# Seven block products instead of eight for the second half of a Mish layer, and two small jobs moved from ScalarE to VectorE

## The chip, the cores and the metric

The kernel runs on one core of one Trainium2 chip. The metric is the device time of one execution in microseconds (us). The kernel before takes 588.06 us, the median of three runs (586.24 to 589.32).

## What is computed

```python
def reference(q, k, v, w_a, w_b, w_out, w_in2, w_out2):   # shortened
    # q, k, v: 2 batches, 8 heads, 576 tokens, 64 per head, float32
    x = softmax(rotate(q) @ rotate(k).T / 8) @ v          # to 1152 tokens x 512
    x = ((x @ w_a) * (x @ w_b)) @ w_out                   # 512 -> 1536 -> 512
    h = x @ w_in2                                         # 512 -> 2048
    g = h * tanh(log1p(exp(min(h, 20))))                  # Mish
    return g @ w_out2                                     # 2048 -> 512
```

## The kernel before

The program has four parts that run into each other: attention of batch 0, attention of batch 1 beside the gated layer of batch 0 (`layer1`, `layer2`), the gated layer of batch 1, and the last layer, which the change is mostly about. Matmuls whose operands need float32 accuracy are done in three passes (`PASSES`): each operand is split into a high and a low part, by a cast or a scaled cast on ScalarE and a subtraction on VectorE, and high x high, high x low and low x high are added up in PSUM.

**The last layer.** The 1152 tokens are two groups: group 0 has 512 tokens, group 1 has 640 (64 of batch 0 and all of batch 1). d_ff = 2048 is cut into 16 tiles `f` of 128. `hidden(g, f)` loads a w_in tile, splits it (ScalarE `w`, VectorE `w`), multiplies it with the split y into a PSUM tile `h` of `h_ps` (two buffers), applies Mish on ScalarE and splits the result into `g`. For group 0 that is 12 matmuls of 512 columns, for group 1 two halves of 320 tokens with 12 matmuls each. `accumulate(g, f)` runs four steps later (`LAG4`): it splits a w_out tile and adds `g` x w_out into PSUM tiles `acc` (six buffers in `acc_ps`), 12 matmuls of 512 columns for group 0 and 15 for group 1. In group 0 the w_out tiles still come as 64-bit words; VectorE turns them into float32 with a shift and two passes (`xw`), and `magnitude` on ScalarE sums the absolute values of each (`junk`, with a read of the accumulator), from which a power of two for w_out's half-precision split in group 1 is made. Tiles converted earlier are kept in DRAM and come back as `wc`.

**The order.** Nothing is issued as it is written. Every call is recorded with a due time (`at`), and `Plan.order` then lists the instructions of each engine by due time and readiness with prices of its own; `any_` lets it choose VectorE or GpSimd. It also keeps VectorE and GpSimd instructions on SBUF operands apart (`lock`). Each engine works through its list strictly in order. All DMAs are issued by SyncE.

**The quotients.** `finish` divides the weighted sums `o` of attention by the softmax denominators `den`. For batch 1 (`p >= NP`) VectorE makes the reciprocals and ScalarE multiplies, two instructions per tile of tokens (`xn`), and two for the rest of 64 tokens (`xbd`).

All traced instructions carry one line (L397, where the plan issues them), so groups are told apart by the names of tiles.

Of the kernel before, what the change touches and what calls it, by code (L numbers as in the profile page):

```python
# [467 lines left out]
def kernel(ctx: ExitStack, tc: tile.TileContext, qk, v5, w1, w2, w34, tab, out):  # L468
# [711 lines left out]

# [22 lines left out]
    acc_t = {}  # L1203

    def hidden(g, f, t0, step):

# [11 lines left out]
        gt = t_p.tile([128, 2, 1280 if g else 640], F16 if g else F32R, tag="g", name=f"g{g}_{f}", bufs=GB)
        for hf in range(nt // hw):
            at(t0 + step * hf * hw / nt)  # L1220
            h = h_ps.tile([128, 512], F32, tag="h", name=f"h{g}_{f}_{hf}")[:, :hw]
# [14 lines left out]
            if g:
                act.activation(gt[:, 0, gs], h, AF.Copy, scale=g_up)
                dve.scalar_tensor_tensor(gt[:, 1, gs], h, g_up, gt[:, 0, gs], op0=ALU.mult, op1=ALU.subtract)
                continue
# [110 lines left out]
```

## Time and profile before

| | |
|---|---|
| median of three runs | 588.06 us |
| profiled execution, span | 588.73 us, 586.9 us |
| TensorE (PE) busy | 562.3 us (96%) |
| VectorE (DVE) busy | 435.1 us (74%) |
| ScalarE (ACT) busy | 380.6 us (65%) |
| GpSimd (POOL) busy | 110.0 us (19%) |
| mean granted TensorE clock | 0.990 of 2.4 GHz |

The span runs from the first to the last instruction of the profiled execution; about 1.8 us of its time lie around it. Busy shares are means over parts with different limits, so the stretches are to be read one by one. An instruction's duration includes some latency that the next one on its engine overlaps, so two neighbours can start closer together than their durations say.

### The profile page before, as it was taken

Reading aid. Unit: us, or ns where it says so; the run is one execution under the profiler, and the core shown is the slowest. Engines: PE = TensorE matmul, PEld = TensorE weight load, DVE = VectorE, ACT = ScalarE, POOL = GpSimd, SP = SyncE. Lnnn points to the kernel's source line nnn. Section 1 sums busy time; section 2 is a strip of 40 time slices with the busy share of each in tenths; the row PEclk is TensorE's granted clock in tenths of the full one; section 3 lists DMA queues with packets and bytes.
Section 4 is the critical chain, followed back from the end, with each engine's and each line's share of the span. In section 5 each row is a group of like instructions: output and inputs, shape, how many; then the busy total and the mean of one; then the engine's idle time right before and its main releaser. Section 6 shows DMA issues by size and latency. Waiting matters only on the chain.

```text
span 586.9 us, 11417 instructions
## 1 busy us (share of the span) xinstructions
PE 562.3 (96%) x4318; PEld 433.8 (74%) x4318; DVE 435.1 (74%) x822; ACT 380.6 (65%) x775; POOL 110.0 (19%) x122
## 2 busy tenths in 40 slices
PE   7899899899998999999999999999989999999997
PEld 5678678798887898889777789965656576655553
DVE  4788999799999989986999999468767625433231
ACT  3889678577776775553876644269999946554430
POOL 3774674415513231200000000000000000000000
PEclk9999999899998999999999999999999999999999
DMA  8246155599997998899999955033763204420002
GB/s 321 85 127 235 55 189 160 159 192 269 266 188 205 266 243 177 190 207 351 402 337 317 291 197 180 6 120 132 263 228 132 90 0 167 158 89 2 1 0 90
DMA packets 84391, 104.02 MB, mean 177 GB/s; under 512 B 51440, under 2 KB 53232, under 8 KB 84336
## 3 DMA queue, kind: packets, MB, share of 16 engines
q1 hardware_dynamic: 84336, 103.29, 58.8%
q8 instruction: 34, 0.56, 0.4%
q14 instruction: 21, 0.17, 0.1%
HBM read 74.94 MB, written 17.04 MB: 157 GB/s over the span
## 4 chain that ended last, share of the span: by engine, by line
PE 66%; ACT 16%; DVE 9%; DMA 4%; issue 3%; POOL 0%; SPq 0%; ACTq 0%; DVEq 0%; POOLq 0%
PE l L397 32%; PE acc L397 11%; PE h L397 9%; PE s L397 6%; ACT L397 5%; PE o L397 4%; DMA pt<-pp 4%; ACT w L397 2%; DVE xw L397 2%; DVE m L397 2%; PE tm L397 2%; ACT junk L397 2%; ACT h L397 1%; ACT g L397 1%; ACT e L397 1%
## 5 line engine op out<-in xcount | busy, mean ns | idle before, releaser
L397 PE MATMUL l<-x,w 128*128 128x320 f32 (+3 forms) x1152 | 160.9, 297 | 2.7 <-DVE a_sb L397 1.8
L397 PEld LDWEIGHTS <-w 128*128 128x128 f16 x1152 | 111.4, 98 | 58.1 <-issue 8.8
L397 DVE SCALAR_TENSOR_TENSOR xw<-wr,xw 128x512 uint32<-128x512 uint32 x160 | 120.1, 759 | 1.2
L397 PE MATMUL acc<-w,g 128*128 128x512 f16 (+1 forms) x432 | 104.6, 393 | 0.0
L397 PE MATMUL h<-y,w 128*128 128x320 f16 (+1 forms) x576 | 99.1, 326 | 3.0 <-DVE g L397 2.4
L397 PEld LDWEIGHTS l<-x,w 128*128 128x128 f32 x576 | 80.2, 195 | 7.8 <-issue 3.4
L397 PE MATMUL l<-ab,w 128*128 128x320 f32 (+1 forms) x576 | 81.8, 298 | 0.1
L397 PEld LDWEIGHTS l<-ab,w 128*128 128x128 f32 x576 | 77.3, 188 | 1.2 <-issue 0.8
L397 DVE TENSOR_REDUCE m<-s 128x1 f32<-128x576 f32 x72 | 51.9, 751 | 12.0 <-PE s L397 11.7
L397 DVE SCALAR_TENSOR_TENSOR w<-wc,w_up,w 128x512 f16<-128x512 f32 x56 | 41.6, 750 | 17.9 <-ACT w L397 17.8
L397 ACT ACTIVATE junk<-xw 128x512 f32<-128x512 f32 x56 | 35.4, 632 | 22.4 <-DVE xw L397 22.1
L397 ACT CAST w<-xw 128x512 fp32r<-128x512 f32 x64 | 39.5, 617 | 15.4 <-DVE xw L397 15.0
L397 PE MATMUL s<-qk 64*128 64x288 f32 x256 | 46.4, 444 | 2.9 <-DVE qk L397 1.5
L397 DVE TENSOR_TENSOR w<-xw,w 128x512 fp32r<-128x512 f32 x50 | 38.5, 770 | 14.0 <-ACT w L397 13.9
L397 ACT ACTIVATE h<-h,h_dn 128x320 f32<-128x320 f32 (+1 forms) x48 | 26.7, 555 | 28.2 <-PE h L397 27.9
L397 ACT ACTIVATE w<-wc,w_up 128x512 f16<-128x512 f32 x56 | 39.5, 716 | 6.4 <-PE l L397 3.0
L397 PEld LDWEIGHTS <-g 128*128 128x128 f16 x240 | 23.5, 98 | 26.4
L397 PEld LDWEIGHTS acc<-w,g 128*128 128x128 f32 x192 | 35.8, 188 | 9.2
L397 DVE SCALAR_TENSOR_TENSOR g<-h,g_up,g 128x320 f16<-128x320 f32 x32 | 17.6, 549 | 29.9 <-ACT g L397 29.9
L397 DVE TENSOR_SCALAR xw<-wr 128x512 uint32<-128x512 uint32 x80 | 35.8, 458 | 1.8 <-DMA wr<-in_w_dram 1.6
L397 PEld LDWEIGHTS s<-qk 64*128 64x128 f32 x256 | 25.3, 190 | 12.1 <-issue 4.8
L397 ACT ACTIVATE s<-s,m 128x576 f32<-128x576 f32 x36 | 25.1, 716 | 12.1 <-DVE m L397 11.6
(134 smaller groups left out, 760.8 us busy)
## 6 DMA issues: line engine op xcount, KB each, us to landing
wr<-in_w_dram SPq DMA_DIRECT2D x80, 512.0 KB, 4.8
wc<-kc SPq DMA_DIRECT2D x48, 256.0 KB, 3.4
kc<-xw SPq DMA_DIRECT2D x32, 256.0 KB, 3.2
qkr<-in_qk_dram SPq DMA_DIRECT2D x14, 576.0 KB, 5.5
ka<-xw SPq DMA_DIRECT2D x24, 256.0 KB, 3.1
wc<-ka SPq DMA_DIRECT2D x24, 256.0 KB, 6.2
v<-in_v_dram SPq DMA_DIRECT2D x12, 320.0 KB, 4.8
out_dram<-o_sb SPq DMA_DIRECT2D x9, 256.0 KB, 2.2
```

The source lines that it names most:

```text
L397: getattr(engine, method)(*map(real, args), **{k: real(v) for k, v in kw.items()})
```

## The change

Three things change.

1. Group 1's hidden layer is made by pairs of w_in tiles (`hidden_two`). With the 640 tokens cut in halves, the 512 rows of k in halves and two tiles of w_in side by side, h is a product of 2 x 2 by 2 x 2 blocks. It is now formed with seven block products and sums of blocks around them. Sums of y blocks are made once, by GpSimd, and split (`token_sums`); sums of w_in blocks are made for each pair by GpSimd (`wx`) and split together with the first tile and half of the second (`wv`). The seven products go to PSUM (`h_ps`, and a new buffer `z_ps` for products 2 and 5), and VectorE adds them up in an SBUF tile `hb`, one copy being ScalarE's. Mish and the split of g then work on 640 tokens at once, from SBUF. `acc_ps` has five buffers instead of six. The scale of y in batch 1 is lowered by four, and g's bound follows.
2. The magnitude of w_out in group 0 is a maximum of absolute values on VectorE (`top`) in place of ScalarE's sum.
3. The quotients of batch 1 are formed on VectorE, one instruction of 128 columns per tile of tokens and two for the rest.

```diff
@@ weights
+            if top is not None:
+                dve.tensor_reduce(top, r, axis=AX.X, op=ALU.max, apply_absolute_value=True)
@@ finish
-        if rest and p >= NP:
-            for i in range(2):
-                r = slice(64 * i, 64 * i + 64)
-                act.activation(xbd[p % 2][r, r], oo[r, i], AF.Copy, scale=den[r, i : i + 1])
-            return
         if rest:
             for i in range(2):
                 r = slice(64 * i, 64 * i + 64)
                 eng.tensor_tensor(xbd[p % 2][r, r], oo[r, i], den[r, i : i + 1].to_broadcast([64, D]), op=ALU.mult)
             return
...
-        if p >= NP:
-            for i in range(2):
-                act.activation(xn_t[p, part][:, c, i], oo[:, i], AF.Copy, scale=den[:, i : i + 1])
-            return
         eng.tensor_tensor(xn_t[p, part][:, c], oo, den.unsqueeze(2).to_broadcast([128, 2, D]), op=ALU.mult)
@@ tile_attention_moe_kernel
-    acc_cm, acc_ps = open_pool("acc_ps", 6, side="right", space=PSUM)
+    acc_cm, acc_ps = open_pool("acc_ps", 5, side="right", space=PSUM)
+    z_cm, z_ps = open_pool("z_ps", space=PSUM)
...
+    def token_sums(t0):
+        def a(r, c):
+            return [y32[1][2 * c + i][:, 0, 320 * r : 320 * r + 320] for i in range(2)]
...
+        for x, y, z, op in (
+            (s1, a(1, 0), a(1, 1), ALU.add),
+            (s2, s1, a(0, 0), ALU.subtract),
+            (s3, a(0, 0), a(1, 0), ALU.subtract),
+        ):
+            for i in range(2):
+                pool.tensor_tensor(x[i], y[i], z[i], op=op)
+        def split(t, i):
+            x = t_p.tile([128, 2, 640], F16, tag=f"sp{i}", name=f"sp{i}")
+            f = t.rearrange("p m n -> p (m n)")
+            act.activation(x[:, 0], f, AF.Copy, scale=y_up[:, 1:2])
+            dve.scalar_tensor_tensor(x[:, 1], f, y_up[:, 1:2], x[:, 0], op0=ALU.mult, op1=ALU.subtract)
+            return x
...
+    def hidden_two(f, t0, step, y):
+        at(t0 - W_LEAD)
+        r = []
+        for i in range(2):
+            x = rings["rawc"][0].tile([128, 512], F32, tag="rawc", name=f"wt{f}_{i}", bufs=rings["rawc"][1])
+            sp.dma_start(x, kept[f"c{2 * (f + i)}"])
+            r.append((x[:, 0:256], x[:, 256:512], x))
+        (b11, b21, b1), (b12, b22, _) = r
+        t = rings["raw"][0].tile([128, 512], I64, tag="raw", name=f"wx{f}", bufs=rings["raw"][1])
...
+        pool.tensor_tensor(t1, b12, b11, op=ALU.subtract)
+        pool.tensor_tensor(t3, b22, b12, op=ALU.subtract)
+        pool.tensor_tensor(t2, b22, t1, op=ALU.subtract)
+        pool.tensor_tensor(t4, b21, t2, op=ALU.subtract)
...
+        for w, x, c in ((wb, b1, slice(0, 512)), (wb, b22, slice(512, 768)), (wt, t, slice(0, 1024))):
+            act.activation(w[:, 0, c], x, AF.Copy, scale=up)
+            dve.scalar_tensor_tensor(w[:, 1, c], x, up, w[:, 0, c], op0=ALU.mult, op1=ALU.subtract)
...
+        def product(k, w, c, a):
+            at(t0 + step * k / 7)
+            ps, tag = (z_ps, "z") if k in (2, 5) else (h_ps, "h")
+            h = ps.tile([128, 512], F32, tag=tag, name=f"h1_{f}_{k}")[:, :320]
+            for i in range(2):
+                for n, (ws, xs) in enumerate(PASSES):
+                    lhsT = w[:, ws, c + 128 * i : c + 128 * i + 128]
+                    pe.matmul(h, lhsT=lhsT, rhs=a(i, xs), start=(i == n == 0), stop=(i == 1 and n == 2))
+            return h
...
+        act.copy(h11, product(0, wb, 0, y_part(0, 0)))
+        add(h12, product(1, wt, 256, s_part(1)), h11)
+        add(h11, product(2, wb, 256, y_part(0, 1)), h11)
+        add(h22, product(3, wt, 512, s_part(2)), h12)
+        add(h21, product(4, wt, 768, y_part(1, 1)), h22)
+        h = product(5, wt, 0, s_part(0))
+        add(h22, h, h22)
+        add(h12, h, h12)
+        add(h12, product(6, wb, 512, s_part(3)), h12)
+        gt = [t_p.tile([128, 2, 1280], F16, tag="g", name=f"g1_{f + i}", bufs=GB) for i in range(2)]
+        for i in range(2):
+            h, g = hb[:, 2 * i : 2 * i + 2].rearrange("p a b -> p (a b)"), gt[i]
+            act.activation(h, h, AF.Mish, scale=dn)
+            act.activation(g[:, 0, 0:640], h, AF.Copy, scale=g_up)
+            dve.scalar_tensor_tensor(g[:, 1, 0:640], h, g_up, g[:, 0, 0:640], op0=ALU.mult, op1=ALU.subtract)
+        return gt
@@ accumulate
-            stat=None if g else 2 * NF1 + NF2 + f,
+            top=None if g else o_sum[:, f : f + 1],
@@ the loop over steps
-            g_t[q] = hidden(*steps[q], T, d)
+            g, f = steps[q]
+            if not g:
+                g_t[q] = hidden(g, f, T, d)
+            elif f % 2 == 0:
+                g_t[q], g_t[q + 1] = hidden_two(f, T, 2 * d, groups[1][3])
+        if q == S_AT:
+            token_sums(T)
```

How the change moves instructions is shown at three places. In the names the number behind a tile's letters is the instance: `h0_6` is the hidden tile 6 of group 0, `h1_0_1` product 1 of pair 0, `wv2` and `wx2` the splits and differences of the pair that begins with tile 2, `xw117` a w_out tile being converted.

On ScalarE, in the middle of group 0, there stood before:

```order
L397 ACT_TABLE_LOAD
L397 ACTIVATE junk44_6042,o_sum_5516<-xw101_6004 128x512
L397 CAST w101_6049<-xw101_6004 128x512
L397 ACT_TABLE_LOAD
L397 ACTIVATE h0_5_0_6020<-h0_5_0_6020,h_dn_5738 128x512
L397 ACTIVATE w106_6060<-wc106_5811,w_up_3543 128x512
L397 CAST g0_5_6068<-h0_5_0_6020 128x512
```

and now:

```order
L397 CAST w99_6077<-xw99_6044 128x512
L397 ACTIVATE h0_6_0_6052<-h0_6_0_6052,h_dn_5721 128x512
L397 ACTIVATE w108_6089<-wc108_5816,w_up_3529 128x512
L397 CAST g0_6_6095<-h0_6_0_6052 128x512
L397 CAST w101_6103<-xw101_6066 128x512
L397 ACTIVATE h0_7_0_6105<-h0_7_0_6105,h_dn_5721 128x512
```

The magnitude and the two table loads around it are gone from the step.

On VectorE, at the end of group 0, there stood before:

```order
L397 TENSOR_TENSOR g0_14_6502<-h0_14_0_6474,g0_14_6502 128x512
L397 TENSOR_TENSOR w121_6515<-xw121_6396,w121_6515 128x512
L397 SCALAR_TENSOR_TENSOR w126_6534<-wc126_6242,w_up_3543,w126_6534 128x512
L397 TENSOR_TENSOR g0_15_6539<-h0_15_0_6513,g0_15_6539 128x512
L397 TENSOR_TENSOR w123_6551<-xw123_6441,w123_6551 128x512
L397 SCALAR_TENSOR_TENSOR g1_0_6572<-h1_0_0_6548,g_up_5876,g1_0_6572 128x320
```

and now:

```order
L397 TENSOR_REDUCE o_sum_4134<-xw117_6459 128x1
L397 TENSOR_TENSOR w117_6488<-xw117_6459,w117_6488 128x512
L397 TENSOR_TENSOR g0_14_6495<-h0_14_0_6451,g0_14_6495 128x512
L397 SCALAR_TENSOR_TENSOR wv2_1_6453<-wx2_6418,two_up_5716,wv2_1_6453 128x1024
L397 TENSOR_SCALAR xw118_6519<-wr118_6468 128x512
L397 SCALAR_TENSOR_TENSOR wv4_0_6502<-wt4_0_6227,two_up_5716,wv4_0_6502 128x512
L397 SCALAR_TENSOR_TENSOR xw118_6519<-wr118_6468,xw118_6519 128x512
L397 TENSOR_TENSOR g0_15_6537<-h0_15_0_6510,g0_15_6537 128x512
L397 SCALAR_TENSOR_TENSOR xw118_6519<-wr118_6468,xw118_6519 128x512
L397 TENSOR_SCALAR xw119_6553<-wr119_6493 128x512
L397 TENSOR_REDUCE o_sum_4134<-xw118_6519 128x1
L397 TENSOR_TENSOR hb0_6580<-h1_0_1_6563,hb0_6580 128x320
```

The reduces and the splits of the pairs 2 and 4 stand among the low parts of g, and the conversion of the last w_out tiles now ends behind the first sum of pair 0.

On VectorE, in the middle of group 1, a pair now looks so (there was one split of g and one of a weight per half before):

```order
L397 TENSOR_TENSOR hb8_7083<-h1_8_4_7136,hb8_7083 128x320
L397 TENSOR_TENSOR hb8_7083<-h1_8_5_7146,hb8_7083 128x320 x2
L397 SCALAR_TENSOR_TENSOR g1_8_7161<-hb8_7083,g_up_6041,g1_8_7161 128x640
L397 SCALAR_TENSOR_TENSOR w129_7178<-wc129_6957,o_up_6781,w129_7178 128x512
L397 TENSOR_TENSOR hb8_7083<-h1_8_6_7175,hb8_7083 128x320
L397 SCALAR_TENSOR_TENSOR wv14_0_7188<-wt14_0_6980,two_up_5716,wv14_0_7188 128x512
L397 SCALAR_TENSOR_TENSOR wv14_0_7188<-wt14_1_6985,two_up_5716,wv14_0_7188 128x256
L397 TENSOR_TENSOR hb10_7201<-h1_10_1_7203,hb10_7201 128x320
```

The splits for pair 14 stand between the sums of two neighbouring pairs.

## Rows read from the trace of the kernel before

**Rows 1.** Windows of each engine, with the columns in the first line.

```profile
core 0: us, PE busy (x) PEld busy (x) DVE busy (x) ACT busy (x) POOL busy (x), PEclk, DMA share, GB/s
388.50:409.00 20.50, 20.50 (x94) 10.95 (x93) 16.95 (x38) 19.58 (x33) 0.00 (x0) 1.00 0.30 98
409.00:466.70 57.70, 55.19 (x241) 34.10 (x241) 39.27 (x65) 56.85 (x86) 0.00 (x0) 1.00 0.55 186
489.40:583.00 93.60, 93.48 (x539) 53.33 (x539) 33.48 (x57) 42.65 (x77) 0.00 (x0) 1.00 0.21 70
120.00:270.00 150.00, 144.86 (x1354) 129.78 (x1353) 139.13 (x261) 99.06 (x225) 41.42 (x35) 0.99 0.95 226
```

**Rows 2.** Timeline of PE in w_in/w_out stage: start us, us, instruction.

```profile
403.60 2.76 PE L397 MATMUL h<-y,w 128*128 128x512 f16 x12
...
409.01 2.76 PE L397 MATMUL h<-y,w 128*128 128x512 f16 x12
...
466.73 1.79 PE L397 MATMUL h<-y,w 128*128 128x320 f16 x12
...
498.29 3.42 PE L397 MATMUL h<-y,w 128*128 128x320 f16 x24
501.55 3.40 PE L397 MATMUL acc<-w,g 128*128 128x512 f16 x15
504.79 3.42 PE L397 MATMUL h<-y,w 128*128 128x320 f16 x24
```

**Rows 3.** Timeline of ACT, one step of group 0.

```profile
447.11 0.66 ACT L397 ACTIVATE h<-h,h_dn 128x512 f32<-128x512 f32 x1
...
448.90 1.28 ACT L397 ACT_TABLE_LOAD   x1
450.19 0.63 ACT L397 ACTIVATE junk<-xw 128x512 f32<-128x512 f32 x1
...
451.44 1.28 ACT L397 ACT_TABLE_LOAD   x1
452.74 0.66 ACT L397 ACTIVATE h<-h,h_dn 128x512 f32<-128x512 f32 x1
```

**Rows 4.** Timeline of DVE, three neighbours in group 0.

```profile
417.27 0.42 DVE L397 TENSOR_SCALAR xw<-wr 128x512 uint32<-128x512 uint32 x1
417.61 1.29 DVE L397 SCALAR_TENSOR_TENSOR xw<-wr,xw 128x512 uint32<-128x512 uint32 x2
418.81 0.75 DVE L397 SCALAR_TENSOR_TENSOR w<-wc,w_up,w 128x512 f16<-128x512 f32 x1
```

**Rows 5.** Groups by form, DVE, 20 to 110 us: xcount | busy us, mean ns.

```profile
L397 DVE SCALAR_TENSOR_TENSOR xw<-wr,xw 128x512 uint32<-128x512 uint32 x11 | 11.9, 1081 | 0.0
...
L397 DVE TENSOR_SCALAR xw<-wr 128x512 uint32<-128x512 uint32 x6 | 4.5, 762 | 0.0
```

**Rows 6.** Groups by form, DVE, 388 to 466 us.

```profile
L397 DVE SCALAR_TENSOR_TENSOR xw<-wr,xw 128x512 uint32<-128x512 uint32 x26 | 17.8, 689 | 0.5
```

**Rows 7.** Groups by form, whole span, GpSimd and DVE.

```profile
L397 POOL TENSOR_TENSOR ab<-a_sb,ab 128x256 fp32r<-128x256 f32 x12 | 10.3, 855 | 42.1 <-ACT ab L397 42.1
...
L397 DVE TENSOR_REDUCE m<-s 128x1 f32<-128x576 f32 x72 | 51.9, 751 | 12.0 <-PE s L397 11.7
...
L397 DVE TENSOR_TENSOR ab<-l,ab 128x320 fp32r<-128x320 f32 x12 | 5.9, 488 | 0.0
...
L397 DVE SCALAR_TENSOR_TENSOR y<-y,y_up 128x320 f16<-128x320 f32 x8 | 4.0, 549 | 0.0
...
L397 DVE SCALAR_TENSOR_TENSOR y<-y,y_up 128x512 f16<-128x512 f32 x4 | 2.7, 746 | 0.0
```

**Rows 8.** Groups by form, ACT, 110 to 270 us; idle before it behind the bar.

```profile
L397 ACT ACTIVATE xn<-o,den 128x64 f32<-128x64 f32 x32 | 8.3, 312 | 6.3 <-DVE den L397 6.2
```

**Rows 9.** Windows as in rows 1, around a drop of the clock.

```profile
180.00:185.00 5.00, 3.58 (x14) 2.08 (x13) 3.79 (x8) 2.44 (x8) 0.89 (x2) 0.81 1.00 302
185.00:190.00 5.00, 5.00 (x36) 5.00 (x35) 5.00 (x9) 3.16 (x6) 0.88 (x1) 0.85 0.46 96
```

More of the change, by code (lines that the diff above doesn't have):

```diff
@@ L425 @@
 LAG4 = 4
+HBB = 2
+S_AT = 0
 GB = 6
@@ L549, in weights @@
     def weights(
-        t, src=None, cached=None, keep=None, split=True, ring=None, hold=0, plain=False, stat=None, scale=None, half=None
+        t, src=None, cached=None, keep=None, split=True, ring=None, hold=0, plain=False, stat=None, top=None, scale=None, half=None
     ):
@@ L1019, in layer2 @@
         if b:
+            dve.tensor_scalar_mul(y_up[:, 1:2], y_up[:, 1:2], 0.25)
+            dve.tensor_scalar_mul(y_dn[:, 1:2], y_dn[:, 1:2], 4.0)
+        if b:
             at(t0 + 24 * dt + Y_LATE)
@@ L1170 @@
     ni = slice(2 * NF1, 2 * NF1 + NF2)
-    h_dn = w_p.tile([128, 2, NF2], F32, tag="h_dn", name="h_dn")
+    h_dn = w_p.tile([128, NF2], F32, tag="h_dn", name="h_dn")
+    two_up = w_p.tile([128, NF2 // 2], F32, tag="two_up", name="two_up")
+    two_dn = w_p.tile([128, NF2 // 2], F32, tag="two_dn", name="two_dn")
     def ahead(j, t):
@@ L1176, in ahead @@
             power(l_ps.tile([128, 512], F32, tag="l", name="w3s")[:, 0:NF2], w_sum[:, ni], w_up[:, ni], w_dn[:, ni])
-            dve.tensor_scalar_mul(h_dn[:, 0, :], w_dn[:, ni], y_dn[:, 0:1])
+            dve.tensor_scalar_mul(h_dn, w_dn[:, ni], y_dn[:, 0:1])
         if j in AHEAD:
@@ L1184 @@
     T += 24 * DT
-    dve.tensor_scalar_mul(h_dn[:, 1, :], w_dn[:, ni], y_dn[:, 1:2])
+    w_two = w_up[:, ni].rearrange("p (f t) -> p f t", t=2)
+    dve.tensor_tensor(two_up, w_two[:, :, 0], w_two[:, :, 1], op=ALU.min)
+    dve.tensor_scalar_mul(two_up, two_up, 0.5)
+    dve.reciprocal(two_dn, two_up)
+    dve.tensor_scalar_mul(two_dn, two_dn, y_dn[:, 1:2])
     dve.tensor_reduce(g_dn, w_up[:, ni], axis=AX.X, op=ALU.min)
-    dve.scalar_tensor_tensor(g_up, g_dn, 2.0**-15, y_up[:, 1:2], op0=ALU.mult, op1=ALU.mult)
+    dve.scalar_tensor_tensor(g_up, g_dn, 2.0**-13, y_up[:, 1:2], op0=ALU.mult, op1=ALU.mult)
     dve.tensor_scalar_min(g_up, g_up, 1e30)
@@ L1199, with new @@
     wo_cm, wo_p = open_pool("wo")
-    acc_cm, acc_ps = open_pool("acc_ps", 6, side="right", space=PSUM)
+    acc_cm, acc_ps = open_pool("acc_ps", 5, side="right", space=PSUM)
+    z_cm, z_ps = open_pool("z_ps", space=PSUM)
     groups = [(0, 512, 512, y0), (512, 640, 320, y1)]
     acc_t = {}
+    sums = []
+    def token_sums(t0):
+        def a(r, c):
+            return [y32[1][2 * c + i][:, 0, 320 * r : 320 * r + 320] for i in range(2)]
+        def new(i):
+            x = t_p.tile([128, 2, 320], F32, tag=f"s{i % 3}", name=f"s{i}")
+            return [x[:, 0], x[:, 1]], x
+        at(t0)
+        s1, t1 = new(0)
+        s2, t2 = new(1)
+        s3, t3 = new(2)
+        for x, y, z, op in (
[11 more added lines that the diff above has]
+            return x
+        sums.extend(split(t, i) for i, t in enumerate((t1, t2, t3)))
+        s4, t4 = new(3)
+        for i in range(2):
+            pool.tensor_tensor(s4[i], a(0, 1)[i], s2[i], op=ALU.subtract)
+        sums.append(split(t4, 3))
@@ new lines, in hidden_two, with y_part, s_part, add @@
+    def hidden_two(f, t0, step, y):
[7 more added lines that the diff above has]
+        t = rings["raw"][0].tile([128, 512], I64, tag="raw", name=f"wx{f}", bufs=rings["raw"][1])
+        t = t.bitcast(F32)
+        t1, t2, t3, t4 = (t[:, 256 * i : 256 * i + 256] for i in range(4))
+        pool.tensor_tensor(t1, b12, b11, op=ALU.subtract)
+        pool.tensor_tensor(t3, b22, b12, op=ALU.subtract)
+        pool.tensor_tensor(t2, b22, t1, op=ALU.subtract)
+        pool.tensor_tensor(t4, b21, t2, op=ALU.subtract)
+        up, dn = two_up[:, f // 2 : f // 2 + 1], two_dn[:, f // 2 : f // 2 + 1]
+        wb, wt = (w_p.tile([128, 2, 1024], F16, tag="w", name=f"wv{f}_{i}", bufs=6) for i in range(2))
+        for w, x, c in ((wb, b1, slice(0, 512)), (wb, b22, slice(512, 768)), (wt, t, slice(0, 1024))):
+            act.activation(w[:, 0, c], x, AF.Copy, scale=up)
+            dve.scalar_tensor_tensor(w[:, 1, c], x, up, w[:, 0, c], op0=ALU.mult, op1=ALU.subtract)
+        hb = t_p.tile([128, 4, 320], F32, tag="hb", name=f"hb{f}", bufs=HBB)
+        h11, h21, h12, h22 = (hb[:, i] for i in range(4))
+        def y_part(r, c):
+            return lambda i, p: y[2 * c + i][:, p, 320 * r : 320 * r + 320]
+        def s_part(j):
+            return lambda i, p: sums[j][:, p, 320 * i : 320 * i + 320]
+        def product(k, w, c, a):
[7 more added lines that the diff above has]
+            return h
+        def add(out, h, x):
+            dve.tensor_tensor(out, h, x, op=ALU.add)
+        act.copy(h11, product(0, wb, 0, y_part(0, 0)))
[8 more added lines that the diff above has]
+        gt = [t_p.tile([128, 2, 1280], F16, tag="g", name=f"g1_{f + i}", bufs=GB) for i in range(2)]
+        for i in range(2):
+            h, g = hb[:, 2 * i : 2 * i + 2].rearrange("p a b -> p (a b)"), gt[i]
[3 more added lines that the diff above has]
+        return gt
@@ L1216, in hidden @@
         )
-        dn = h_dn[:, g, f : f + 1]
-        gt = t_p.tile([128, 2, 1280 if g else 640], F16 if g else F32R, tag="g", name=f"g{g}_{f}", bufs=GB)
+        dn = h_dn[:, f : f + 1]
+        gt = t_p.tile([128, 2, 640], F32R, tag="g", name=f"g{g}_{f}", bufs=GB)
         for hf in range(nt // hw):
@@ L1235, in hidden @@
             act.activation(h, h, AF.Mish, scale=dn)
[L1236 to L1239, printed above, removed]
             act.copy(gt[:, 0, gs], h)
@@ L1291 @@
         T += d
-    for cm in (h_cm, acc_cm, t_cm, c_cm, wo_cm, x_cm, w_cm, d_cm):
+    for cm in (z_cm, h_cm, acc_cm, t_cm, c_cm, wo_cm, x_cm, w_cm, d_cm):
         close_pool(cm)
```

## The prediction

> **What bounds the kernel now.** I read the windows first, then the order in time of TensorE, ScalarE and VectorE in the stage that multiplies by w_in and w_out, then the groups by form for prices. Four stretches matter [rows 1]. From 409.0 to 466.7 us (group 0, the first 512 tokens) ScalarE is busy 56.85 of 57.70 us and VectorE 39.27. From 489.4 to the last matmuls (group 1, the other 640 tokens) TensorE is busy 93.48 of 93.60 us, with VectorE at 33.48 and ScalarE at 42.65. In the second batch's attention (120 to 270 us) TensorE has 144.86 and VectorE 139.13 of 150 us: two engines close to full.
>
> Group 0 is paced by ScalarE. One step, from Mish to Mish, is 452.74 - 447.11 = 5.63 us, and it holds two table loads of 1.28 us, one on each side of the w_out magnitude (0.63 us) [rows 3]. Where nothing held TensorE its step was 409.01 - 403.60 = 5.41 us [rows 2]. Group 1 is paced by TensorE: 24 matmuls of 320 columns from 498.29 to 501.55, so 0.136 us each, then 15 of 512 columns to 504.79, so 0.216 us each [rows 2]; a pair of tiles takes 2 x 6.50 = 13.0 us.
>
> **Prices on VectorE.** An instruction holds the engine for its duration less about 0.09 us: two passes of 0.69 us start and end within 418.81 - 417.61 = 1.20 us, so 0.60 each, and the 0.42 us shift holds it for 0.34 us [rows 4, 6]. A two-source product with a scalar costs 0.549 us at 320 columns and 0.746 at 512 [rows 7], about 1.03 ns a column; that gives 0.48 us at 256, 0.88 at 640, 1.27 at 1024, so 0.39, 0.79 and 1.18 us of the engine. The new reduce over 512 columns is not in the trace; from the one of 576 columns (0.751 us, [rows 7]) I take 0.68, or 0.60 of the engine. An add out of PSUM at 320 columns is 0.488 us [rows 7], 0.40 of the engine.
>
> **Group 0 (term A).** ScalarE loses the magnitude and both table loads in each step, so it no longer paces. If TensorE did, the ten steps from 409.01 would take 54.1 us and group 1's first product would start at 463.1 instead of 466.73 [rows 2]: -3.6 us. But the order shows what VectorE must do between the low part of g of tile 4 and that of tile 15: 24 passes of 0.60 on w_out's words (14.4), 12 shifts (4.1), 11 new reduces (6.6), 22 low parts of w_out and g (13.2), 8 of w_in at 0.66 (5.3), seven splits for the first pairs (three of 512, two of 256, two of 1024 columns: 5.1), and small ones (1.5): 50.2 us. The stretch before, 388.5 to 409.0, has 3.55 us of VectorE free [rows 1] and receives four splits of 640 columns (3.2 us), so I let it end as before, at 409. The second product waits for a buffer that the g of tile 15 frees: 459.2 at the earliest. To this comes GpSimd. While GpSimd works, VectorE's passes over SBUF are longer: 1.081 us against 0.689, and the shift 0.762 against 0.42 [rows 4 to 6]. Three pairs of weight differences fall into this stretch, 12 instructions of 256 columns, 0.855 us in the mean [rows 7], about 9.2 us of GpSimd less the same overlap; if all of it pushes VectorE aside, the product starts at 468.4. TensorE wants it at 463.1 + 0.8 = 463.9; before, the same place was 467.5. So A lies between -3.6 and +0.9; I take -1.5, near the middle, since neither end has a row of its own.
>
> A rule of the Trainium skill bears on that middle. The row first: a one-source shift is lengthened too [rows 4, 5]. The page "SBUF — State Buffer", section "Who interferes with whom", says that VectorE and GpSimd share one pair of ports as an exclusive lock, that an instruction with two SBUF inputs or in a two-port mode takes it, and that tensor_reduce never contends on trn2. The lengthened passes and shifts agree with the lock; no run here shows the reduce. By the rule the 11 reduces could run beside GpSimd and A would move towards -3.6; if reduces were blocked as the shift is, towards +0.9.
>
> **Group 1, fewer matmuls (term B).** Seven products of 6 matmuls replace 48 per pair: 6 x 0.136 = 0.81 us for each of 8 pairs, 48 matmuls, -6.5 us. TensorE then needs 42 x 0.136 + 30 x 0.216 = 12.2 us a pair. VectorE needs 7 adds (2.8), splits of 512, 256 and 1024 columns (2.2), two w_out low parts (1.3) and two low parts of g at 640 columns (1.6): 7.9 us, and with four GpSimd differences (3.1) 11.0 us. That is hidden in 12.2, with little to spare; without this cover each pair would cost the difference.
>
> **The first pairs of group 1 (term C).** Here VectorE still has the last w_out tiles. Between the second product and group 1's first accumulation TensorE has 16 products (13.0) and 48 wide matmuls at 5.41 / 24 = 0.225 (10.8): 23.8 us. VectorE has 20.5 us by the same count (16 adds, six splits, three low parts of g, two w_out tiles, the output copies), and eight GpSimd differences 6.2 us: 26.7. The adds stand in that queue behind splits, and a product waits for the add that frees its PSUM buffer (two buffers and one). Bounds 0 and +5 (3 us from the sum, 2 for adds that arrive late); I take +2. That PSUM for the sums shrinks from 6 to 5 buffers costs nothing here: four are in use in group 0, and the copies that free them stand on VectorE and ScalarE before the first accumulation that needs them.
>
> **Attention of the second batch (term D).** ScalarE loses 32 products of 0.312 us and 6.3 us of waiting before them [rows 8], and 8 small ones. VectorE gets 16 of 128 columns (about 0.2 us of the engine, from 0.488 at 320 columns less the 1.03 ns a column) and 8 of 64, 4.3 us, and one rotary product from GpSimd, and gives two residuals to it: +3.8 us net on an engine at 139 of 150. TensorE's own idle time there is 5.1 us [rows 1]. So D is between -3 (most of that idle time goes) and +4 (VectorE's load lands on the path). The planner writes the rest of that stage in a new order too, which no row prices. I take 0.
>
> **Sum.** -1.5 - 6.5 + 2 + 0 = -6.0. The profiled execution took 588.73 us (span 586.9 and 1.8 around it), 0.67 above the median of 588.06. From the median: 582.0 us. Own range of this case 578.5 to 585.0.
>
> **Rivals.**
> 1. VectorE keeps up everywhere. For it: 50.2 us of work in 54.1 us of TensorE. Against it: GpSimd's lock and waits for ScalarE. A -3.6, B -6.5, C 0, D -1: 577.0.
> 2. VectorE takes ScalarE's place as the pacer of group 0 and of the first pairs, and gives the matmuls' gain back. For it: 59 us with GpSimd against 54. Against it: some of VectorE's work there reads PSUM and has not been seen to wait. A +0.9, B -6.5, C +5, D 0: 587.5.
> 3. Slower: the VectorE cycle of a pair paces group 1. With full durations it is 7 x 0.488 + 2.5 + 2 x 0.75 + 2 x 0.88 = 9.2 us, four GpSimd instructions at 0.855 make it 12.6, and a wait for Mish of each half (0.66 us at 512 columns [rows 3], an estimated 0.83 at 640) 14.3. Against 13.0 before that is +1.3 in each of the six pairs that carry conversions, +7.8, with A at +0.9: 596.8. It decides once a pair takes VectorE over 13.0 us. Against it: the overlap in [rows 4], and the last pairs' slack.
>
> **How the numbers follow.** Forecast 0.55, rival 1 0.17, rival 2 0.16, rival 3 0.12. A measurement of this kernel tells about 0.5% from no change: 585.1 to 591.0 is the same. Faster: forecast and rival 1, 0.72; same: rival 2, 0.16; slower: rival 3, 0.12. The range, 575.5 to 590.0, holds the forecast, rival 2 and rival 1 but for its low tail, and leaves out rival 3. D widens both ends; a drop of TensorE's clock like the one at 180 to 190 us (granted 0.81 and 0.85 [rows 9]) costs 10 x 0.17 = 1.7 us and can go or come with the new order.
>
> **What would show it.** Right: no table load in group 0 but the first, its steps near 5.4 us, VectorE over 90% busy there, group 1's first products near 466, pairs of 12.2 us behind them, attention ending within 3 us of before. Wrong: TensorE waiting for VectorE's adds beyond the third pair (rival 3), steps of group 0 above 5.6 us (rival 2), a new pause with a clock drop between 120 and 270 us (D).

## The result, and the profile after

The changed kernel takes 578.54 us, the median of four runs (575.43 to 581.27), beside 587.35 us of the kernel before, also four runs. The ratio is 0.9851 with a 95% interval of 0.9808 to 0.9894. The prediction had 582.0 us: right in sign, 3.5 us too slow, inside its range and at the lower edge (578.5) of the range that it calls its own case. The four runs of the one program go with the granted clock: spans of 573.7, 576.3, 577.3 and 579.5 us at 0.999, 0.990, 0.990 and 0.988. The profiled one is the longest, 581.27 us with a span of 579.5, and is compared with the profiled one before (586.9).

The engines' busy time in the page after:

```profile
PE 555.2 (96%) x4270; PEld 429.7 (74%) x4270; DVE 483.0 (83%) x918; ACT 339.3 (59%) x669; POOL 147.7 (25%) x163
```

VectorE gained 48 us of work and ScalarE lost 41. Windows after, with the columns of [rows 1]: most of group 0, the first pairs of group 1, the rest of group 1, attention of batch 1.

```profile
412.17:466.01 53.84, 53.84 (x241) 33.39 (x239) 51.60 (x84) 25.70 (x43) 11.27 (x12) 1.00 0.61 210
466.01:491.30 25.29, 25.29 (x154) 18.44 (x154) 21.33 (x39) 13.40 (x21) 6.17 (x8) 1.00 0.25 86
491.30:575.43 84.13, 84.13 (x476) 46.27 (x473) 51.94 (x83) 40.88 (x58) 10.92 (x12) 1.00 0.20 60
120.00:270.00 150.00, 144.22 (x1359) 131.17 (x1358) 141.53 (x284) 88.72 (x185) 42.80 (x36) 0.99 0.95 227
```

In the last layer TensorE is now busy in every one of these microseconds; ScalarE, full in group 0 before, is at 25.70 of 53.84. TensorE's timeline:

```profile
455.21 2.76 PE L397 MATMUL h<-y,w 128*128 128x512 f16 x12
...
460.61 2.76 PE L397 MATMUL h<-y,w 128*128 128x512 f16 x12
...
466.01 0.99 PE L397 MATMUL h<-y,wv 128*128 128x320 f16 x6
...
518.17 0.98 PE L397 MATMUL h<-y,wv 128*128 128x320 f16 x6
...
530.45 0.98 PE L397 MATMUL h<-y,wv 128*128 128x320 f16 x6
```

A step of group 0 is 5.40 us, a pair of group 1 530.45 - 518.17 = 12.28. ScalarE's timeline of one such step has no table load, and a wait of 3.22 us for TensorE in front of Mish, where [rows 3] had two loads:

```profile
452.61 0.66 ACT L397 ACTIVATE h<-h,h_dn 128x512 f32<-128x512 f32 x1 [3.22 <-PE h L397]
453.30 0.59 ACT L397 CAST g<-h 128x512 fp32r<-128x512 f32 x1
454.04 1.15 ACT L397 ACTIVATE wv<-wx,two_up 128x1024 f16<-128x1024 f32 x1
```

One place got worse, the maximum over batch 0's y, from which y's scale is made (VectorE's and ScalarE's rows, then TensorE's):

```profile
277.85 1.41 DVE L397 SCALAR_TENSOR_TENSOR w<-wc,w_up,w 128x512 f16<-128x512 f32 x2
277.97 0.63 ACT L397 ACTIVATE junk<-xw 128x512 f32<-128x512 f32 x1 [0.52 <-DVE xw L397]
...
278.59 0.41 ACT L397 COPY y<-l 128x320 f32<-128x320 f32 x1
...
279.18 0.48 DVE L397 TENSOR_REDUCE y_mx<-l 128x1 f32<-128x320 f32 x1
...
279.91 0.15 DVE L397 TENSOR_REDUCE y_m<-y_mx 128x1 f32<-128x8 f32 x1
...
280.12 0.38 PE L397 MATMUL ys<-eye,y_m 128*1 128x128 f32 x2 [2.16 <-DVE y_m L397]
```

On VectorE two weight splits stand in front of `y_mx`, on ScalarE a magnitude in front of y's copy. TensorE waits 2.16 us, and in the windows the clock (the third number from the end) falls behind the wait:

```profile
275.00:280.00 5.00, 2.96 (x24) 2.35 (x22) 4.93 (x10) 3.42 (x7) 0.00 (x0) 1.00 1.04 402
280.00:285.00 5.00, 4.88 (x26) 3.12 (x27) 4.67 (x12) 3.10 (x7) 0.00 (x0) 0.68 1.02 389
```

Four marks on TensorE part the difference of the two profiled executions (us):

| from ... to | before | after | difference |
|---|---|---|---|
| start ... end of batch 0's gated layer | 277.09 | 276.22 | -0.9 |
| ... product for w_in's scale (`w3s`) | 99.92 | 103.78 | +3.9 |
| first product of group 0 ... of group 1 | 79.95 | 76.24 | -3.7 |
| ... end of the last matmul | 116.14 | 109.42 | -6.7 |

That is -7.4 in all, the difference of the spans (from `w3s` to the first product of group 0 both take 9.77 us).

### The profile page after: what moved, and what is told of

Same layout as the page of the kernel before. It is cut to its first block, busy times and chain, and to the rows that moved or that the text cites. A ratio compares the mean times of both kernels' runs of the same rounds, so it can differ in the third digit from the quotient of the medians.

```text
span 579.5 us, 11387 instructions
## 1 busy us (share of the span) xinstructions
PE 555.2 (96%) x4270; PEld 429.7 (74%) x4270; DVE 483.0 (83%) x918; ACT 339.3 (59%) x669; POOL 147.7 (25%) x163
## 4 chain that ended last, share of the span: by engine, by line
PE 76%; DVE 10%; DMA 7%; ACT 4%; issue 2%; SPq 0%; DVEq 0%; ACTq 0%
PE l L397 30%; PE acc L397 17%; PE h L397 15%; PE s L397 6%; DMA pt<-pp 5%; PE o L397 5%; DVE xw L397 3%; DVE m L397 2%; PE tm L397 2%; DVE w L397 1%; DMA wc<-ka 1%; ACT e L397 1%; ACT vhl L397 1%; DMA qkr_q<-in_qk_dram 1%; PE xt L397 1%
## 5 line engine op out<-in xcount | busy, mean ns | idle before, releaser
L397 PEld LDWEIGHTS <-w 128*128 128x128 f16 x768 | 74.4, 99 | 38.0 <-issue 4.0
L397 PEld LDWEIGHTS <-wv 128*128 128x128 f16 x336 | 32.4, 98 | 17.3 <-issue 2.7
L397 PE MATMUL h<-y,w 128*128 128x512 f16 x192 | 44.2, 380 | 0.0
L397 DVE TENSOR_SCALAR xw<-wr 128x512 uint32<-128x512 uint32 x80 | 40.5, 512 | 0.4 <-DMA wr<-in_w_dram 0.4
L397 DVE TENSOR_TENSOR w<-xw,w 128x512 fp32r<-128x512 f32 x48 | 36.0, 751 | 1.4 <-ACT w L397 1.4
L397 ACT ACTIVATE w<-wc,w_up 128x512 f16<-128x512 f32 x40 | 28.4, 718 | 13.3 <-DMA wc<-ka 6.6
L397 ACT ACTIVATE junk<-xw 128x512 f32<-128x512 f32 x40 | 25.3, 632 | 17.0 <-DVE xw L397 15.7
L397 DVE TENSOR_TENSOR hb<-h,hb 128x320 f32<-128x320 f32 x56 | 26.0, 485 | 8.8 <-PE h L397 6.5
L397 POOL TENSOR_TENSOR w<-xw,w 128x512 fp32r<-128x512 f32 x16 | 20.7, 1294 | 49.6 <-ACT w L397 44.4
L397 DVE SCALAR_TENSOR_TENSOR w<-wc,w_up,w 128x512 f16<-128x512 f32 x40 | 29.5, 748 | 3.8 <-ACT w L397 3.8
```

Source lines behind the costliest of these rows:

```text
L397: getattr(engine, method)(*map(real, args), **{k: real(v) for k, v in kw.items()})
```

## The experiments

Every run is set beside runs of the kernel before on the same chip, 585.9 to 587.3 us in the median. The first four are each part alone, and all but the quotients.

**Magnitude alone** (the kernel before with `top`):

```diff
-            stat=None if g else 2 * NF1 + NF2 + f,
+            top=None if g else o_sum[:, f : f + 1],
```

> Only w_out's magnitude moves to VectorE. Theory 1 (the three parts add up, each by its own stage): group 0's steps fall from 5.63 to 5.41 us, no table load in them, the stage starts its second group 3.6 us earlier, total about 583.7 against 587.4. Rival (the step is held by something else, TensorE's waits or the DMA of w_out): steps stay above 5.55 us and the total within 1 us of before.

583.05 us, ratio 0.9925 [0.9910, 0.9939]. Group 0 takes 76.23 us instead of 79.95 in the profiled executions; that is 3.7 of the 4.3 us gained against 587.32.

**Quotients alone** (the kernel before, in `finish`):

```diff
-        if rest and p >= NP:
...
-        if p >= NP:
-            for i in range(2):
-                act.activation(xn_t[p, part][:, c, i], oo[:, i], AF.Copy, scale=den[:, i : i + 1])
-            return
```

> Only the second batch's quotients move to VectorE. Theory 1 (VectorE's extra 3.8 us lands on the path of that stage, as the +3.0 us of the profiled changed kernel would say): about 590.4, 3 us slower than before. Rival (the +3.0 us comes from pauses of TensorE that the new order happens to have, not from VectorE's load): within 1.5 us of before, with other pauses in the profile.

588.24 us, ratio 1.0023 [1.0005, 1.0041]: +0.9 us against 587.32. Nothing is gained; the rival with a small effect was nearer.

**Seven products alone** (the changed kernel with magnitude and quotients on ScalarE as before):

```diff
+        if p >= NP:                                     # and so the block for rest
+            for i in range(2):
+                act.activation(xn_t[p, part][:, c, i], oo[:, i], AF.Copy, scale=den[:, i : i + 1])
+            return
...
-            top=None if g else o_sum[:, f : f + 1],
+            stat=None if g else 2 * NF1 + NF2 + f,
```

> Only the seven products; magnitude and quotients stay on ScalarE. Theory 1: group 1 gains 6.5 to 6.7 us, but ScalarE, which still paces group 0, gets the splits of the sums and of the first pairs there (about 7 more instructions, 4 to 6 us), so group 0 becomes longer by 2 to 5 us: total 582 to 585. Rival (ScalarE's new work fits into its queue without cost): 580.7.

589.53 us, ratio 1.0043 [1.0024, 1.0063]: slower than before, a miss. VectorE's and TensorE's waits from 388 to 500 us (us in total, how many, the longest) and the windows from 409 to 495:

```profile
DVE g L397 <- ACT g L397: 11.8, 11, 3.3
...
PE h L397 <- DVE g L397: 10.2, 6, 4.7
```

```profile
409.00:470.00 61.00, 54.68 (x242) 34.08 (x241) 45.49 (x71) 56.31 (x85) 12.09 (x14) 1.00 0.55 189
470.00:495.00 25.00, 21.12 (x111) 15.43 (x110) 15.44 (x26) 13.78 (x20) 5.92 (x7) 0.86 0.10 32
```

ScalarE was full in group 0 already. The splits for pairs (1.14 us for a `wv` of 1024 columns) come on top of it between the table loads, the high parts of g come late from ScalarE and the low parts from VectorE behind them, and TensorE waits 10.2 us in all, once for 4.7; over the 25 us from 470 its clock is 0.86 in the mean. The 48 matmuls are gone, but more is lost in front of them.

**All but the quotients** (the changed kernel with the first four lines of that diff alone, and the block for rest):

> The changed kernel with the quotients back on ScalarE. Theory 1 (the parts add up, quotients cost 3 us): 576 to 577, about 2 to 3 us faster than the changed kernel's 578.5. Rival (quotients are neutral, the pauses are chance): within 1 us of 578.5.

576.75 us, ratio 0.9813 [0.9790, 0.9837]. The parts don't add: -4.3, +0.9 and +2.2 make -1.2. On top of the magnitude's move the seven products bring 576.75 - 583.05 = -6.3, without it +2.2. The quotients on top of both cost some 0.6 to 2.8 us, by the ratios of the changed kernel and of three kernels below whose edits leave its time as it is (0.9824 to 0.9860 beside 0.9813); the intervals overlap, so that sign and size rest on the quotients alone, above.

**What of the magnitude paced group 0?** The kernel before with the sum over a copy instead of absolute values, still on ScalarE:

```diff
-        act.activation(junk, r, AF.Abs, accum_out=total)
+        act.activation(junk, r, AF.Abs if col < n else AF.Copy, accum_out=total)
```

> The kernel before with w_out's magnitude still on ScalarE, summed over a copy in place of absolute values (so the scale of w_out is made from another number), a function that needs no table load beside Mish. It parts the two costs that moving the magnitude took away together. Theory 1, the two table loads of 1.28 us in a step paced group 0, not the magnitude's 0.63 us and its read of 0.19: ScalarE falls to 31 to 35 us of the stretch, group 0 takes 76.2 us instead of 79.9 and the time is 583.0 us (582.0 to 584.0), as with the magnitude on VectorE. Rival, its place between Mish and the cast of g delays TensorE by itself: 77.5 to 79 us, 584.5 to 586.5.

582.67 us, ratio 0.9942 [0.9919, 0.9965]; group 0 takes 76.23 us. ScalarE's timeline and window (as above):

```profile
443.10 0.66 ACT L397 ACTIVATE h<-h,h_dn 128x512 f32<-128x512 f32 x1 [1.99 <-PE h L397]
...
444.76 0.64 ACT L397 ACTIVATE junk<-xw 128x512 f32<-128x512 f32 x1
445.30 0.20 ACT L397 ACTIVATION_READ_ACCUMULATOR junk<-xw 128x1 f32 x1
...
448.50 0.66 ACT L397 ACTIVATE h<-h,h_dn 128x512 f32<-128x512 f32 x1 [1.99 <-PE h L397]
```

```profile
404.90:461.90 57.00, 57.00 (x255) 35.74 (x253) 41.44 (x68) 33.33 (x68) 0.00 (x0) 1.00 0.56 194
```

The magnitude is still there, 0.64 us and a read of 0.20, and group 0 takes what it takes without it: the two table loads were the whole price.

**How much room has VectorE in group 0?** Each maximum over a w_out tile taken twice, then four times:

```diff
             if top is not None:
                 dve.tensor_reduce(top, r, axis=AX.X, op=ALU.max, apply_absolute_value=True)
+                dve.tensor_reduce(top, r, axis=AX.X, op=ALU.max, apply_absolute_value=True)
```

> The changed kernel with every maximum over a w_out tile taken twice, to find how much room VectorE has in group 0. Theory 1: VectorE is busy 51.8 of 54.0 us there and TensorE paces, so 11 more reduces of 0.60 us push VectorE's work to about 58 us; group 0 grows from 76.2 to 79.5 to 81.5 us with waits of TensorE for the low parts of g, and the time is 582.5 us (580.5 to 584.5). Rival: VectorE's busy time overstates its load (its neighbours overlap by 0.09 us) and the reduces find room: group 0 stays below 77.0 us and the time within 1 us of 578.5.

577.20 us, ratio 0.9824 [0.9800, 0.9848]; group 0 still 76.24 us: theory 1 fell. The windows of group 0 and of the rest of group 1, and VectorE's reduces in group 0:

```profile
411.42:465.26 53.84, 53.84 (x241) 33.38 (x239) 51.22 (x87) 24.96 (x42) 7.98 (x8) 1.00 0.58 192
...
490.55:574.70 84.15, 84.15 (x479) 46.74 (x478) 56.49 (x90) 41.70 (x60) 11.08 (x12) 1.00 0.21 64
```

```profile
L397 DVE TENSOR_REDUCE o_sum<-xw 128x1 f32<-128x512 f32 x20 | 13.5, 677 | 0.0
```

Nine more reduces stand there (20; the changed kernel has 11) and VectorE is no busier (51.22 us): other work moved out, and 4.5 us more are done in the rest of group 1. Part of what VectorE does beside group 0 is not due there.

> The changed kernel with every maximum over a w_out tile taken four times, to find where VectorE begins to pace; twice cost nothing, since other work of VectorE moved into group 1. Theory 1, what counts is the work that is due by a date: up to 491 us VectorE is busy 90.3 of 101.6 us, 13 tiles with three more reduces of 0.60 us make it 114, and only some 5 us of splits for later pairs can move behind, so TensorE waits for the low parts of g and the w_out tiles: 5 to 10 us, 583 to 588 us. Rival: still room, under 580 us.

590.26 us, ratio 1.0080 [1.0051, 1.0109]: theory 1, and over its range (583 to 588). Windows of group 0 and of the 35 us behind it:

```profile
411.10:465.00 53.90, 53.90 (x243) 33.19 (x242) 51.72 (x91) 22.92 (x39) 3.47 (x4) 1.00 0.48 161
465.00:500.00 35.00, 26.92 (x137) 17.55 (x137) 34.69 (x62) 13.64 (x21) 11.10 (x14) 0.95 0.33 105
```

Even now TensorE does not wait up to 465; the debt falls due behind it, where VectorE is full and TensorE idles 8.1 of 35 us.

**What does GpSimd's lock cost?** The differences of w_in blocks on VectorE:

```diff
-        pool.tensor_tensor(t1, b12, b11, op=ALU.subtract)
+        dve.tensor_tensor(t1, b12, b11, op=ALU.subtract)    # and so t2, t3, t4
```

> The changed kernel with the 32 differences of w_in blocks on VectorE in place of GpSimd. Theory 1: GpSimd holds VectorE up by far less than its own time (3 of 11.3 us in group 0). 12 differences of 256 columns at 0.33 to 0.4 us of VectorE come in there and 3 us of lengthened passes go: VectorE is busy 52.5 to 54 of the 54 us from 412 to 466, the passes over w_out's words are back at 0.69 us, group 0 takes 76.2 to 77.5 us and the time is 579.0 us (578.0 to 580.5). Rival, as the prediction's middle had it: GpSimd's whole time is taken from VectorE, so VectorE falls to 47 to 49 us there; time 577.5 to 578.5.

577.46 us, ratio 0.9836 [0.9802, 0.9870]: no change in time, under theory 1's range and at the rival's edge. What parts the two is VectorE's busy time in group 0, the window of which is

```profile
408.73:462.57 53.84, 53.84 (x241) 33.38 (x239) 52.77 (x96) 26.22 (x44) 0.00 (x0) 1.00 0.65 215
```

so 52.77 us, as theory 1 had it, and not 47 to 49. That alone would not part them, since the planner fills the stretch (as with the maxima taken twice); the durations do. VectorE's groups there, of the changed kernel first, then of this one:

```profile
L397 DVE SCALAR_TENSOR_TENSOR xw<-wr,xw 128x512 uint32<-128x512 uint32 x24 | 17.5, 739 | 0.0
L397 DVE TENSOR_TENSOR w<-xw,w 128x512 fp32r<-128x512 f32 x11 | 7.9, 719 | 0.3 <-ACT w L397 0.3
...
L397 DVE TENSOR_REDUCE o_sum<-xw 128x1 f32<-128x512 f32 x11 | 7.5, 677 | 0.0
...
L397 DVE TENSOR_SCALAR xw<-wr 128x512 uint32<-128x512 uint32 x11 | 5.3, 485 | 0.0
L397 DVE SCALAR_TENSOR_TENSOR wv<-wt,two_up,wv 128x512 f16<-128x512 f32 x3 | 3.2, 1057 | 0.0
```

```profile
L397 DVE SCALAR_TENSOR_TENSOR xw<-wr,xw 128x512 uint32<-128x512 uint32 x25 | 16.7, 685 | 0.0
L397 DVE TENSOR_TENSOR w<-xw,w 128x512 fp32r<-128x512 f32 x12 | 8.2, 684 | 0.3 <-ACT w L397 0.2
L397 DVE TENSOR_REDUCE o_sum<-xw 128x1 f32<-128x512 f32 x12 | 8.1, 679 | 0.0
...
L397 DVE TENSOR_SCALAR xw<-wr 128x512 uint32<-128x512 uint32 x12 | 5.1, 421 | 0.0
...
L397 DVE SCALAR_TENSOR_TENSOR wv<-wt,two_up,wv 128x512 f16<-128x512 f32 x2 | 1.5, 747 | 0.0
```

Beside 11.27 us of GpSimd VectorE was lengthened by 24 x 0.054 + 11 x 0.035 + 11 x 0.064 + 3 x 0.31 = 3.3 us, not by 11. These are means; most of the instructions never met GpSimd. The changed kernel's timeline of one pair's differences:

```profile
436.69 1.18 POOL L397 TENSOR_TENSOR wx<-wt,wt 128x256 f32<-128x256 f32 x1 [35.64 <-DVE xw L397]
...
437.19 0.68 DVE L397 TENSOR_REDUCE o_sum<-xw 128x1 f32<-128x512 f32 x1
...
438.13 0.69 DVE L397 TENSOR_TENSOR g<-h,g 128x512 fp32r<-128x512 f32 x1 [0.26 <-ACT g L397]
438.53 1.87 POOL L397 TENSOR_TENSOR wx<-wt,wx 128x256 f32<-128x256 f32 x2
438.74 1.08 DVE L397 TENSOR_TENSOR w<-xw,w 128x512 fp32r<-128x512 f32 x1
```

Eight instructions of VectorE that met GpSimd in group 0 are longer, like the low part of w here (1.08 us, else 0.68). A low part of g, which reads PSUM, and the reduce are not, which is part of why GpSimd's whole time is not VectorE's loss. The three reduces of w_out tiles that met GpSimd, here and in the first pairs, each took 0.68 us, as without it (679 ns). The Trainium skill's "SBUF — State Buffer", section "Who interferes with whom", says that on trn2 tensor_reduce never contends with GpSimd; the trace agrees.

**Is the third PSUM buffer for products what lets the adds come late?**

```diff
-            ps, tag = (z_ps, "z") if k in (2, 5) else (h_ps, "h")
+            ps, tag = (h_ps, "h")
```

> The changed kernel with all seven products in the two PSUM buffers that the halves had before; the third buffer is left unused. Theory 1: the third buffer is what lets VectorE's adds come late without a wait of TensorE. A product takes 0.81 us, the add that frees its buffer 0.49 us and stands behind splits of 0.7 to 1.2 us, so TensorE waits for adds in each pair: 0.3 to 0.6 us, 2.5 to 5 us in all, pairs of 12.6 to 12.9 us, 582.0 us (581.0 to 583.5). Rival: the order keeps other matmuls between the products and VectorE is free enough: pairs of 12.27 us as now, 578.0 to 579.5.

577.93 us, ratio 0.9860 [0.9832, 0.9889]: the rival. The window of the rest of group 1:

```profile
486.75:571.00 84.25, 84.25 (x477) 46.41 (x476) 52.20 (x84) 40.38 (x58) 11.11 (x12) 1.00 0.19 56
```

TensorE is never idle there, and no wait for an add stands in the first pairs either: for two buffers the planner writes a new order, with accumulations behind every one or two products in the rest of group 1 (in the changed kernel up to four products stand in a row), and an add is done before its buffer is wanted. So this run shows that two buffers suffice, not that the changed kernel's own order would do with them.

**The wait for y's maximum.** Three edits of the changed kernel's order alone; `behind` takes the instruction of an engine that writes a tile, with whatever waits for it, and puts it behind the one that is named by its output and input:

```diff
         self.done = self.order()
+        self.behind("act", "junk24", "y0_3", "l2_0_3_1")   # magnitude behind y's copy
+        self.behind("dve", "w41", "y_mx", "l2_0_3_1")      # two splits behind y_mx
+        self.behind("dve", "w43", "y_mx", "l2_0_3_1")
```

> The changed kernel with three instructions put later: on ScalarE one magnitude (the one at 277.97 us) behind the copy of the last tile of y of batch 0, on VectorE the splits of two weight tiles (277.85 us) behind that tile's maximum. Theory 1: the quotients cost nothing up to the end of attention (TensorE stands at 271.8 us in both kernels) but shift the maximum of y behind those three, TensorE waits 2.16 us for it and the clock falls to 0.68 for 5 us. Then the wait shrinks to 0.3 to 0.8 us, the clock stays at 1.00 between 280 and 285, the product for w_in's scale starts near 377.5 instead of 380.0, and the time is 576.0 us (575.0 to 577.0). Rival: the quotients' own load on VectorE, or a clock that differs from run to run, is the cause: 578.0 to 579.0 and 379.5 to 380.5.

577.35 us, ratio 0.9843 [0.9819, 0.9866], between the two theories. VectorE's timeline:

```profile
275.64 0.48 DVE L414 TENSOR_REDUCE y_mx<-l 128x1 f32<-128x320 f32 x1
...
276.04 1.41 DVE L414 SCALAR_TENSOR_TENSOR w<-wc,w_up,w 128x512 f16<-128x512 f32 x2
...
277.70 0.15 DVE L414 TENSOR_REDUCE y_m<-y_mx 128x1 f32<-128x8 f32 x1
```

The first maximum is early, and the second waits behind the splits: TensorE waits 1.10 us. So they went behind the second, with a shift:

```diff
-        self.behind("dve", "w41", "y_mx", "l2_0_3_1")
-        self.behind("dve", "w43", "y_mx", "l2_0_3_1")
+        self.behind("dve", "w41", "y_m", "y_mx")
+        self.behind("dve", "w43", "y_m", "y_mx")
+        self.behind("dve", "xw39", "y_m", "y_mx")
```

> The changed kernel with the maximum over y of batch 0 put ahead of what stood in front of it: on ScalarE one magnitude goes behind the copy of y's last tile, on VectorE two weight splits and a shift go behind both maxima (the edit before moved them behind the first alone, and the second then waited for them). In the kernels with the quotients on VectorE TensorE waited there for 0.81, 1.06, 1.10, 1.19, 1.90 and 2.16 us, and the way from the end of batch 0's last tile to the product for w_in's scale took 100.7, 101.0, 101.05, 101.1, 103.4 and 103.8 us, against 99.9 where there was no wait. Theory 1, the order in the queues makes the wait: it falls under 0.4 us, that way takes 99.9 to 100.3 us, the clock stays at 1.00, and the time is 576.3 us (575.3 to 577.3). Rival, a weight reload that lands late holds ScalarE in front of the copy: the wait stays at 0.8 to 1.2 us and the time at 577.5.

577.62 us, ratio 0.9860 [0.9832, 0.9888]. The time is the rival's, the mechanism neither's: the wait went on to the third maximum. TensorE's rows:

```profile
276.38 0.38 PE L415 MATMUL ys<-eye,y_m 128*1 128x128 f32 x2 [0.29 <-DVE y_m L415]
...
278.83 0.38 PE L415 MATMUL ys<-y_row,ones_w 1*128 1x1 f32 x2 [1.28 <-DVE y_row L415]
```

Last, the splits behind the third:

```diff
-        self.behind("dve", "w41", "y_m", "y_mx")
-        self.behind("dve", "w43", "y_m", "y_mx")
+        self.behind("dve", "w41", "y_row", "ys0")
+        self.behind("dve", "w43", "y_row", "ys0")
```

> The changed kernel with the two weight splits put behind the whole chain of maxima of batch 0's y (the last of them, over one row, included), the shift behind the second maximum and one magnitude of ScalarE behind the copy of y. With the splits between the second and the third maximum TensorE's wait had only moved on: 0.29 us for the second, 1.28 us for the third. Theory 1, the queue's order alone makes these waits: together they fall under 0.6 us, the way from the end of batch 0's last tile to the product for w_in's scale takes 99.9 to 100.3 us, no clock loss there, 576.3 us (575.3 to 577.3). Rival: the splits are now late for their own products and the wait moves on once more; that way stays over 100.7 us, 577.6 us.

576.21 us (575.30 to 578.92), ratio 0.9839 [0.9811, 0.9867]. TensorE's waits from 272 us to the end:

```profile
PE ys L415 <- DVE y_m L415: 0.5, 2, 0.4
```

The second is for the other batch; here 0.39 us are left and the clock stays at 1.00. The way to `w3s` is 100.5 us, 0.2 over what was expected and 0.6 over the kernels without a wait. It is the shortest profiled span of all, 574.1 us, but by the times it can't be told from the changed kernel (the intervals overlap), nor from the one without the quotients.

The marks of these kernels side by side, each of its profiled execution (us):

| kernel | batch 0's layer ends | TensorE's wait for maxima | way from there to `w3s` |
|---|---|---|---|
| before | 277.09 | none | 99.9 |
| magnitude alone | 275.77 | none | 99.9 |
| all but the quotients | 276.19 | none | 100.0 |
| two buffers | 274.71 | 0.81 | 100.7 |
| quotients alone | 274.96 | 1.06 | 101.0 |
| `y_mx` early | 275.07 | 1.10 | 101.05 |
| differences on VectorE | 275.45 | 1.19 | 101.1 |
| maxima twice | 275.86 | 1.90 | 103.4 |
| changed kernel | 276.22 | 2.16 | 103.8 |
| maxima four times | 276.76 | 2.24 | 102.2 |
| `y_m` early | 274.36 | 0.29 + 1.28 | 101.6 |
| `y_row` early | 274.13 | 0.39 | 100.5 |

"Two buffers" and "differences on VectorE" have the changed kernel's order up to there, instruction by instruction. Their waits of 0.81 and 1.19 us against its 2.16 are chance from run to run, and go with how long ScalarE waits for reloaded weights in front of the maxima: 5.4, 5.6 and 6.6 us in two waits. With `y_row` early ScalarE waits 6.3 us there and TensorE 0.39: in that order late weights hardly reach TensorE.

Up to 1.28 us TensorE's waits there cost about themselves; the two of 1.90 and 2.16 cost 3.5 and 3.9, since the clock falls behind them. The longest, 2.24 us with the maxima four times, cost 2.2 and left the clock at 1.00, so the length of a wait alone does not say whether the clock falls. The windows from 280 to 285 us with the maxima twice, then four times:

```profile
280.00:285.00 5.00, 5.00 (x28) 3.27 (x27) 3.45 (x11) 2.97 (x6) 0.00 (x0) 0.66 1.05 408
```

```profile
280.00:285.00 5.00, 4.00 (x31) 2.91 (x32) 4.88 (x14) 3.97 (x9) 0.00 (x0) 1.00 1.02 399
```

## Why the prediction was right or wrong

**Term A, group 0: -1.5 forecast, -3.7 measured, its floor.** That ScalarE's pacing goes and that the steps are TensorE's was right, and it was the table loads alone. Mis-sized was the time at which group 1 can start, and two steps of it failed. "If all of it pushes VectorE aside" charged GpSimd's 9.2 us to VectorE; the lengthening was 3.3. And everything that stands in VectorE's list between two low parts of g was counted as due there; with the maxima taken twice, the planner moves splits and conversions behind the group and TensorE does not wait. The middle between the two ends had no row behind it, and the lower end was the truth.

**Term B, 48 matmuls: -6.5 forecast, B and C together -6.7 measured.** The pair came to 12.28 us (12.2 forecast). But the gain depends on A: without the magnitude's move the same edit makes the kernel 2.2 us slower. The prediction added A and B as if each stood alone; since both were done here, the sum held.

**Term C, the first pairs: +2 forecast, 0 measured.** VectorE is busy 21.33 of 25.29 us there, beside 6.17 of GpSimd, where 26.7 had been added up, again with GpSimd's whole time; and the late adds that it feared don't hold TensorE, even with one buffer fewer and an order made for that.

**Term D, batch 1's attention: 0 forecast, +3.0 in the profiled execution, +0.9 by the quotients alone.** The bounds of -3 and +4 held it, the place was not the one that was priced. With the quotients on VectorE attention ends no later: batch 0's layer ends at 275.3 us in the mean of the nine kernels here that have them (274.1 to 276.8), at 276.1 in the five without (275.6 to 277.1); a gain of 0.8 us is not settled by that. What costs in the traces is the new order of the instructions behind it, "which no row prices", at a chain of three small maxima that TensorE waits for in all nine kernels with the quotients on VectorE and in none of the five without, and a clock that falls behind that wait in two of the nine. By the times this is not settled: with the wait nearly gone the kernel can't be told from the changed one.

**The sum.** That it came near is in part luck: A, B and C were put 4.4 us too dear together, D 0.9 to 3.0 us too cheap.

**Rivals.** Rival 1 (VectorE keeps up everywhere) has the mechanism of the last layer right: -3.6 and -6.5, C nothing. At 577.0 us it is also nearer to the median than the forecast; it missed D. Rival 2 (VectorE paces) is what happens with the maxima four times, but only in the first pairs: group 0 keeps TensorE full even then. Rival 3 (the cycle of a pair) is far off: VectorE is at 51.94 of 84.13 us.

What was to show it did: steps near 5.4 us, VectorE over 90% (51.60 of 53.84), group 1 at 466.0, pairs of 12.3. Of the signs of being wrong one came, for D: "a new pause with a clock drop", at 278 us, behind the stretch that was named.

## What to carry to other kernels

Two table loads around a small function can pace a stage: look at which functions alternate on ScalarE before moving work, since another function may do. An engine at 95% is not yet the pacer: ask what of its work is due in the stretch, since a planner lets the rest slide until, as with the maxima four times, the debt comes due elsewhere. Gains of parts don't add when one part takes the room that another needs: run each alone and all but one. And a chain of tiny instructions that feeds TensorE is moved by any edit that reorders the queue in front of it; freeing one link only moved the wait to the next here, until all three were free.

## What the runs showed of the hardware

- A table load of 1.28 us stood on both sides of the sum of absolute values beside Mish, 23 from 385 to 480 us; with a sum over a copy in its place one was left.
- TensorE's clock after a wait: at the maxima of batch 0's y waits of 0.81 to 1.28 us left it at 1.00 in the window from 280 to 285 us. After waits of 1.90 and 2.16 us its mean was 0.66 and 0.68 there, between its levels of 1.2 and 2.4 GHz; after one of 2.24 us it was 1.00.
- VectorE's instructions that met a difference on GpSimd in group 0: passes of 0.68 us took 0.98 to 1.22, shifts of 0.42 took 0.63 and 0.94, splits of 512 columns of 0.75 took 1.21 and 1.22. Over the whole stretch, where most met none, the means grew by 5 to 8% (passes), 15% (shifts) and 42% (three splits). Reduces and low parts of g read from PSUM kept their 0.68 and 0.69 us.
